# A transformer block with adaptive layer norm on one core: first loads in a new order, constant matmuls ahead of the first transposes, tiles turned through two banks, and a new shift table

## Chip, core and metric

The kernel runs on one core of a Trainium2 chip. Its time is the device time of one execution in microseconds (us). Before the change three runs gave 738.66, 738.86 and 739.36 us, a median of 738.86 us. The engines are called PE (TensorE, matrix products), DVE (VectorE), ACT (ScalarE), POOL (GpSimd) and SP (SyncE, which here only issues transfers). PEld is the loading of weights into PE.

## What is computed

The reference, cut to what matters (x is 2048 x 1024, all inputs are bfloat16):

```python
mod = (silu(c) @ w_mod).reshape(1, 6, 1, -1)
sa, ca, ga, sb, cb, gb = mod[:, 0] ... mod[:, 5]
h = layernorm(x) * (1 + ca) + sa
q, k, v = split(h @ wqkv)                 # 32 heads of 32
pq, pk = phi(q), phi(k)                   # phi(t) = t + 1 where t > 0, else exp(t); + 1e-6
o = (pq @ sum(pk^T v)) / (pq . sum(pk))   # linear attention
x = x + ga * (o @ wo)
h = layernorm(x) * (1 + cb) + sb
x = x + gb * ((gelu(h @ w_gate) * (h @ w_up)) @ w_down)
```

## The kernel before

The 2048 rows are worked in four blocks of 512, each of four tiles of 128 rows. The attention half takes the blocks in turn for k and v (`kvq_phase`, L1396) and then q, merges, and the feed-forward half takes two groups of 1024 rows. Many products are done by Strassen-like schemes with seven half products.

**A planner orders everything.** Each call on `te`, `ve`, `ac`, `gp`, `sy` only records an operation. `Plan.order` (L439) estimates start times with a cost model, forward and backward, and gives each operation a due time. PE's operations stay in program order; those of the other engines are ordered by due time, and loads are not issued more than a set time ahead of theirs. Two lists bend the due times: `plan.chain` and `plan.pairs` hold operations of which each must not be due before its predecessor. `plan.aim` ties an operation to a transfer. `Plan.refine` (L466) then applies the table `SHIFTS` (L20): for every engine a list of numbers, where position i of the final order takes the operation at position i + shift of the planner's. `zN` stands for N zeros. So a table fits only the list of operations that it was made for.

**The start** is `start_phase` (L936). It works block 0 without the scratch that the later blocks use:

- It loads four tiles of x (`load_x`, L780: 256 KB each), the columns of `w_mod` for ca in four quarters (`wm`, L947: 512 KB each, into `wm_ca`), the v columns of `wqkv` in four quarters (`wv` through L784, 512 KB each), the sa columns of `w_mod` (`ModRow`, L832: four of 512 KB), and the first half of the k columns `Wk` (L784, 1 MB). Before the change x1, x3 and one quarter of `wm_ca` go out on ACT's queue, as does c (L775), the rest on SP's.
- c is transposed on PE (L976) with `identb` (L974, a copy on DVE) and goes through silu to `scol`, a column for PE, and `srep`.
- The tiles are normalized: tiles 0 and 2 with bn_stats on DVE (`ln_rows`: L865, L867, then Ln and Exp on ACT, L878 and L879, and the scaling L894), tiles 1 and 3 with sums on ACT (`act_stats`: L884 to L887, and L991 on DVE).
- `start_tile` (L903) turns a tile with eight PE transposes (L906). The two halves of it go to two PSUM banks and are copied to `hs0` by DVE (L909) and ACT (L910). Two pairs of banks are used in turn, from a ring of four (`psT`).
- `scale_cols` (L927) makes 1 + ca for half of the channels with 32 products of one column each (L931), and L934 adds the 1. `scale_wv` (L912) multiplies a half or quarter of Wv by it (L914). I call the two halves' products SC0 and SC1.
- `v_plain` (L917) makes the v products of tile tl and column half n, in two halves over k (L922). I call them V with tile and column half, so V10 is tile 1, columns 0. L925 copies the results to `vta`.
- The row of sa is made by `ModRow.step` (L859) and turned to a column by `columns` (L845 to L852). Then hr1[0], the modulated input of the k products, is made with eight DVE operations, one for each slice of 128 channels (L1033).
- `keep_warm` (L898) issues matmuls whose result nobody reads.

After it `shift_row` (L1037) makes a row from sa and Wv (L859 again), and the k products of block 0 follow (`k_group`, L1249).

**Block 1** comes from `ln1_block(1)` (L1054): x4 to x7 are loaded, normalized (stats on DVE at L865, POOL at L872 to L1063, ACT at L1065), stored to a DRAM scratch (L1066, on POOL's queue), turned by a DMA transpose (L1067, on SP's queue) and scaled by DVE (L1070). It is recorded after `start_phase`. Before the change its loads are put into `plan.chain` among those of the start. Its v products are L1150, its k products L1249.

PE's order before the change, read from its table: transpose of c, tile 1, two `keep_warm`, tile 0, first half of SC0, tile 2, second half of SC0, V10, tile 3, V20, first half of SC1, V00, V30, V01, second half of SC1, and the other V products. The second half of V11 (L922 at 43.47) comes only among the k products.

Of the kernel before, what the change touches and what calls it, by code (L numbers as in the profile page):

```python
# [21 lines left out]
        "z1 40 40 40 40 40 40 40 40 48 48 -10 -10 -10 -10 -10 -10 -10 -10 -10 -10 -10 -10 -10 -10 -10 -10 -10 -10 -10 "  # L22
        "-10 -10 -10 -10 -10 18 18 18 18 10 10 10 10 -18 -18 -18 -18 -18 -18 -18 -18 -18 -18 -18 -18 -18 -18 -18 -18 4 "
        "4 4 4 16 16 16 16 8 8 8 8 -4 -4 -4 -4 12 12 12 12 12 12 12 12 12 12 12 12 12 12 12 12 -32 -32 -32 -32 24 24 24 "
        "24 -28 -28 -28 -28 z16 4 4 4 4 -40 -40 -40 -40 8 8 8 8 8 8 8 8 -4 -4 -4 -4 -12 -12 -12 -12 24 24 24 24 4 4 4 4 "
        "4 4 4 4 4 4 4 4 4 4 4 4 -20 -20 -20 -20 4 4 4 4 4 4 4 4 4 4 4 4 20 20 20 20 20 20 20 20 20 20 20 20 20 20 20 "
        "20 20 20 20 20 20 20 20 20 -12 -12 -12 -12 -12 -12 -12 -12 12 12 12 12 12 12 12 12 -36 -36 -36 -36 -36 -36 -36 "
        "-36 20 20 20 20 20 20 20 20 -4 -4 -4 -4 -4 -4 -4 -4 -96 -96 -96 -96 -8 -8 -8 -8 -8 -8 -8 -8 z8 16 16 16 16 16 "
        "16 16 16 16 16 16 16 16 16 16 16 -16 -16 -16 -16 -16 -16 -16 -16 8 8 8 8 48 48 48 48 -24 -24 -24 -24 -24 -24 "
        "-24 -24 -4 -4 -4 -4 -4 -4 -4 -4 33 33 33 33 28 3 3 3 3 3 3 3 3 11 11 11 11 -21 -21 -21 -21 -21 -21 -21 -21 -21 "  # L30
        "-21 -21 -21 8 8 8 8 33 33 33 33 33 33 33 33 z8 13 13 13 13 5 5 5 5 -41 -41 -41 -41 -41 -41 -41 -41 -11 -11 -11 "
        "-11 -19 -19 -19 -19 -24 16 16 16 16 16 16 16 16 16 16 16 16 16 16 16 16 -16 -16 -16 -16 -16 -16 -16 -16 -16 "
        "-16 -16 -16 -16 -16 -16 -16 4 4 4 4 36 36 36 36 z12 24 24 24 24 -24 -24 -24 -24 -8 -8 -8 -8 -8 -8 -8 -8 24 24 "
        "24 24 -12 -12 -12 -12 -12 -12 -12 -12 -12 -12 -12 -12 32 32 32 32 24 24 24 24 16 16 16 16 -8 -8 -8 -8 z4 -24 "
        "-24 -24 -24 -24 -24 -24 -24 -8 -8 -8 -8 -20 -20 -20 -20 28 28 28 28 -4 -4 -4 -4 16 16 16 16 -8 -8 -8 -8 -4 -4 "
        "-4 -4 -12 -12 -12 -12 -8 -8 -8 -8 8 8 8 8 8 8 8 8 -4 -4 -4 -4 4 4 4 4 8 8 8 8 -28 -28 -28 -28 -4 -4 -4 -4 4 4 "
        "4 4 -4 -4 -4 -4 4 4 4 4 -4 -4 -4 -4 z20 24 24 24 24 -4 -4 -4 -4 -4 -4 -4 -4 -4 -4 -4 -4 4 4 4 4 20 20 20 20 "
        "-12 -12 -12 -12 -12 -12 -12 -12 12 12 12 12 28 28 28 28 20 20 20 20 -16 -16 -16 -16 -16 -16 -16 -16 -16 -16 "
        "-16 -16 20 20 20 20 -12 -12 -12 -12 -12 -12 -12 -12 -12 -12 -12 -12 32 32 32 32 -8 -8 -8 -8 -8 -8 -8 -8 16 16 "
        "16 16 -8 -8 -8 -8 -4 -4 -4 -4 z4 36 36 36 36 -20 -20 -20 -20 z12 8 8 8 8 -32 -32 -32 -32 4 4 4 4 20 20 20 20 "  # L40
        "-16 -16 -16 -16 z4 -20 -20 -20 -20 z4 -8 -8 -8 -8 4 4 4 4 -4 -4 -4 -4 4 4 4 4 52 52 52 52 52 52 52 52 52 52 52 "
        "52 -16 -16 -16 -16 -8 -8 -8 -8 -16 -16 -16 -16 -12 -12 -12 -12 -12 -12 -12 -12 -12 -12 -12 -12 -12 -12 -12 -12 "
        "-12 -12 -12 -12 -12 -12 -12 -12 -12 -12 -12 -12 -12 -12 -12 -12 -12 -12 -12 -12 -12 -12 -12 -12 8 8 8 8 8 8 8 "
        "8 8 8 8 8 -12 -12 -12 -12 28 28 28 28 28 28 28 28 12 12 12 12 -8 -8 -8 -8 -8 -8 -8 -8 -8 -8 -8 -8 -8 -8 -8 -8 "
        "16 16 16 16 16 16 16 16 16 16 16 16 16 16 16 16 -56 -56 -56 -56 -24 -24 -24 -24 24 24 24 24 12 12 12 12 20 20 "
        "-22 -22 -22 -22 -30 -30 -30 -30 -6 -6 -6 -6 16 16 16 16 16 16 16 16 16 16 16 16 16 16 16 16 -8 -8 -8 -8 -8 -8 "
        "-8 -8 -38 -38 -38 -38 13 3 3 3 3 7 2 2 2 2 8 8 8 8 18 -1 -1 -1 -1 3 -50 -50 -50 -50 4 4 4 4 5 -5 -5 -5 -5 1 1 "
        "1 1 -14 14 -1 -1 -1 -1 1 1 1 1 6 z4 -10 -10 z4 6 6 6 6 6 6 6 6 -8 -8 -8 -8 -8 2 -9 -1 4 4 4 4 -4 -4 -4 -4 2 2 "
        "2 2 -4 -4 z4 40 40 40 40 40 40 40 40 24 24 24 24 24 24 24 24 48 48 48 48 48 48 48 48 24 24 24 24 24 24 24 24 "
        "24 24 24 24 24 24 24 24 -40 -40 -40 -40 -40 -40 -40 -40 -40 -40 -40 -40 -40 -40 -40 -40 -40 -40 -40 -40 -40 "  # L50
        "-40 -40 -40 -40 -40 -40 -40 -40 -40 -40 -40 z16 16 16 16 16 16 16 16 16 -8 -8 -8 -8 -8 -8 -8 -8 -8 -8 -8 -8 -8 "
        "-8 -8 -8 8 8 8 8 8 8 8 8 -8 -8 -8 -8 -8 -8 -8 -8 16 16 16 16 4 4 4 4 4 4 4 4 -12 -12 -12 -12 -12 -12 -12 -12 8 "
        "8 8 8 8 8 8 8 -8 -8 -8 -8 -8 -8 -8 -8 8 8 8 8 8 8 8 8 -8 -8 -8 -8 -8 -8 -8 -8 4 4 4 4 4 4 4 4 4 4 4 4 -12 -12 "
        "-12 -12 40 40 40 40 40 40 40 40 16 16 16 16 16 16 16 16 -12 -12 -12 -12 -20 -20 -20 -20 -16 -16 -16 -16 -16 "
# [449 lines left out]
def kernel(  # L504
# [14 lines left out]
    P = 128  # L519
# [1674 lines left out]
```

## Time and profile before

| what | value |
|---|---|
| median of the runs | 738.86 us |
| span of the profiled execution, first to last instruction | 737.0 us |
| median less span | 1.86 us |
| PE busy | 719.7 us (98%) |
| DVE busy | 652.0 us (88%) |
| ACT busy | 453.9 us (62%) |
| bytes moved | 159.27 MB, 216 GB/s |
| chain that ended last | PE 79%, DVE 14%, ACT 3% |

The profile is of one execution; its times count from the start of the span. No time of that execution outside its span is given, so the span is set beside the median of the runs. A group of instructions is named by the line that issued it, its engine and its operation; L787 is a helper (`tt_op`) that many steps share. The chain of work that ended last is followed back from the last instruction, each step to what released it. "Waits" are idle times of an engine before an instruction that another one released. Some records can be missing.

### The profile page before, as it was taken

The page shows a single profiled execution, that of the slowest core. Times are in us where ns is not written, and L with a number is a line of the kernel's source. Part 1 is how long each engine was busy: PE and PEld are TensorE (multiplying, and loading weights), DVE is VectorE, ACT ScalarE, POOL GpSimd, SP SyncE. Part 2 cuts the span into 40 slices and gives each one's busy share as a digit, 9 for nine tenths or more (in the row PEclk, how much of TensorE's full clock was granted, in tenths as well). Part 3 has the DMA queues.
Part 4 walks back from the last instruction along what each step waited for, and adds up shares of the span by engine and source line. Part 5 has one row for each costly group of instructions (what it writes and reads, how often), then busy time and mean ns, then how long its engine had stood idle before and what let it go on. Part 6 is the DMA issues. An engine that isn't in the chain of part 4 may idle for free.

```text
span 737.0 us, 12105 instructions
## 1 busy us (share of the span) xinstructions
PE 719.7 (98%) x4340; PEld 406.1 (55%) x4353; DVE 652.0 (88%) x1466; ACT 453.9 (62%) x827; POOL 98.6 (13%) x174
## 2 busy tenths in 40 slices
PE   4999999999999999999999999999999999999997
PEld 3444545444444455555555667555555555568774
DVE  6699898777799999999997598988897999999998
ACT  5377566569786889999876631026777776642010
POOL 2344471000020222112110000010000000000000
PEclk9999999999999999999999999999999999999999
DMA  9987994978698967655896897745343545698972
GB/s 315 356 215 222 222 185 112 325 277 223 199 212 245 320 223 242 203 161 209 235 237 217 242 282 242 244 148 177 107 125 114 172 136 180 196 283 248 284 236 73
DMA packets 160958, 159.27 MB, mean 216 GB/s; under 512 B 34177, under 2 KB 140417, under 8 KB 160257
## 3 DMA queue, kind: packets, MB, share of 16 engines
q1 hardware_dynamic: 142864, 121.52, 55.2%
q0 software_dynamic: 14848, 33.82, 15.3%
q10 hardware_dynamic: 3184, 3.15, 1.3%
q8 instruction: 34, 0.56, 0.3%
q14 instruction: 28, 0.22, 0.1%
HBM read 122.42 MB, written 36.04 MB: 215 GB/s over the span
## 4 chain that ended last, share of the span: by engine, by line
PE 79%; DVE 14%; ACT 3%; issue 2%; DMA 1%; POOL 0%; ACTq 0%; DVEq 0%; POOLq 0%
PE psum L1706 28%; DVE mem L787 12%; PE psum L1717 9%; PE psum L1922 7%; PE psum L1150 7%; PE psum L1220 7%; PE psum L1967 5%; PE psum L1527 4%; PE psum L1249 4%; PE psum L1591 3%; PE psum L922 2%; PE psum L1264 1%; ACT mem L1094 1%; DVE mem L2139 1%; DMA ts<-mem 1%
## 5 line engine op out<-in xcount | busy, mean ns | idle before, releaser
L787 DVE TENSOR_TENSOR mem<-mem 128x256 f16<-128x256 f16 (+13 forms) x857 | 376.8, 485 | 15.4 <-ACT mem L1791 3.3
L1706 PE MATMUL psum<-mem 128*128 128x512 f16 x1144 | 273.0, 379 | 0.1
L1094 ACT ACTIVATE mem<-psum 128x512 f32<-128x512 f32 (+3 forms) x320 | 168.1, 556 | 138.3 <-DVE mem L787 42.0
L787 DVE TENSOR_TENSOR mem<-psum,mem 128x512 f16<-128x512 f32 (+6 forms) x213 | 159.4, 756 | 31.3 <-PE psum L1220 4.9
L1706 PEld LDWEIGHTS <-mem 128*128 128x128 f16 (+1 forms) x1144 | 111.7, 98 | 104.3 <-issue 1.7
L1717 PE MATMUL psum<-mem 128*128 128x256 f16 x742 | 105.4, 272 | 0.1
L1717 PEld LDWEIGHTS <-mem 128*128 128x128 f16 (+1 forms) x742 | 72.4, 98 | 41.4 <-issue 1.3
L1967 PE MATMUL psum<-mem 128*128 128x256 f16 (+1 forms) x784 | 88.5, 273 | 0.1
L1967 PEld LDWEIGHTS <-mem 128*128 128x128 f16 x784 | 76.7, 98 | 12.7 <-issue 0.5
L1922 PE MATMUL psum<-mem 128*128 128x512 f16 (+2 forms) x348 | 75.7, 370 | 1.6 <-DVE mem L787 1.5
L1150 PE MATMUL psum<-mem 128*128 128x512 f16 (+1 forms) x274 | 62.7, 379 | 0.3
L787 DVE TENSOR_TENSOR psum<-psum,mem 128x256 f32<-128x256 f32 x106 | 44.4, 427 | 15.5 <-ACT mem L1094 13.9
L1922 PEld LDWEIGHTS <-mem 128*128 128x128 f16 x350 | 34.2, 98 | 37.0 <-issue 1.7
L1762 ACT ACTIVATE psum<-psum 128x512 f32<-128x512 f32 x56 | 32.7, 585 | 34.0 <-PE psum L1706 22.5
L1220 PE MATMUL psum<-mem 128*128 128x512 f16 x224 | 51.9, 379 | 0.0
L1150 PEld LDWEIGHTS <-mem 128*128 128x128 f16 x280 | 27.0, 98 | 31.0 <-issue 0.2
L1781 ACT ACTIVATE mem<-psum 128x512 f16<-128x512 f32 x56 | 33.3, 597 | 8.7 <-PE psum L1706 8.6
L1220 PEld LDWEIGHTS <-mem 128*128 128x128 f16 (+1 forms) x224 | 21.6, 98 | 26.1 <-issue 1.4
L1791 ACT ACTIVATE mem<-mem 128x512 f16<-128x512 f16 x56 | 34.8, 628 | 0.9 <-DVE mem L787 0.9
L1249 PE MATMUL psum<-mem 128*128 128x512 bf16 x123 | 28.5, 379 | 0.3
L1527 PE MATMUL psum<-mem 128*128 128x512 f16 x128 | 28.1, 379 | 0.0
L1328 POOL DMA_DIRECT2D ts<-in_B_w_down_dram x28 | 27.2, 1411 | 3.7 <-DMA ts<-in_B_w_down_dram 3.7
(142 smaller groups left out, 562.8 us busy)
## 6 DMA issues: line engine op xcount, KB each, us to landing
mem<-in_B_w_gate_dram SPq DMA_DIRECT2D x14, 1024.0 KB
mem<-in_B_w_up_dram SPq DMA_DIRECT2D x14, 1024.0 KB
mem<-in_w_mod_dram SPq DMA_DIRECT2D x23, 512.0 KB
mem<-us SPq DMA_DIRECT2D x24, 448.0 KB
mem<-ts SPq DMA_DIRECT2D x5, 1792.0 KB
ts<-in_B_w_down_dram POOLq DMA_DIRECT2D x28, 256.0 KB, 5.8
mem<-in_B_w_down_dram SPq DMA_DIRECT2D x15, 448.0 KB
mem<-in_A_x_dram SPq DMA_DIRECT2D x22, 256.0 KB
```

The lines of the kernel that those rows point to most:

```text
L787: ve.tensor_tensor(out=out, in0=a, in1=b, op=op)
L1094: ac.activation(out=t, in_=ps, func=AF.Copy)
L1150: te.matmul(ps, lhsT=A[:, k, i * P:(i + 1) * P], rhs=B[:, k, :], start=(start and k == 0), stop=(k == KH - 1), skip_group_check=True)
L1220: te.matmul(o, lhsT=W[:, k, (j0 + i) * P:(j0 + i + 1) * P], rhs=h_form(a, k), start=(start and k == 0), stop=(k == KH - 1), skip_group_che ...
L1249: te.matmul(ps, lhsT=hr1[b][:, k, tl * P:(tl + 1) * P], rhs=Wk[:, k, n * NW:(n + 1) * NW], start=(k == 0), stop=(k == KD - 1))
L1527: te.matmul(psw[:, half, :], lhsT=pqT[b][:, g, tl * P:(tl + 1) * P], rhs=Wp[:, g, half * NW:(half + 1) * NW], start=(g == 0), stop=(g == K ...
L1706: te.matmul(ps, lhsT=a[:, k, e, :], rhs=b[:, k, :], start=(start and k == 0), stop=(k == KH - 1), skip_group_check=True)
L1717: te.matmul(ps, lhsT=self.x[a][:, k, :], rhs=self.y[y][:, k, :], start=(start and k == 0), stop=(k == KH // 2 - 1), skip_group_check=True)
L1781: ac.activation(out=o, in_=ps, func=AF.Gelu_apprx_tanh)
L1791: ac.activation(out=o, in_=o, func=AF.Gelu_apprx_tanh)
L1922: te.matmul(psm[:, q, c], lhsT=A[:, i, q * P:(q + 1) * P], rhs=wt[:, i, c], start=(start and i == 0), stop=(i == NPR - 1), skip_group_chec ...
L1967: te.matmul(ps[:, q, :], lhsT=a[:, k, q * P:(q + 1) * P], rhs=y[:, k, :], start=(start and q == 0 and k == 0), stop=(k == NPR // 2 - 1), s ...
```

## The change

- `SHIFTS` is replaced for all five engines: PE has 4365 entries for 4353, DVE 1451 for 1453, ACT 805 for 804, POOL 153 as before, SP 224 for 223.
- Loads: the program order is now x0, x1, two quarters of `wm_ca`, one of Wv, x2, one of Wv, x3, the other two of `wm_ca`, the other two of Wv, sa, Wk, and then x4 to x7 (`first_x`), which `ln1_block(1)` takes over. x1 and x2 go out on ACT's queue, everything else on SP's, with c on ACT's as before. All entries in `plan.chain` and `plan.pairs` go, and the `plan.aim` of the start.
- `keep_warm` now multiplies the identity with itself, four copies side by side, so it needs no data. There are 8 of them ahead of the transpose of c, 4 ahead of tile 0 and 2 after it in the program (14 in all, 2 before), into bank 5 in place of bank 6.
- `start_tile` uses banks 0 and 1 for every tile. The banks of the V products change.
- The program order of the products changes, and tile 0 comes first. PE's order by the new table: 8 `keep_warm`, transpose of c, 6 `keep_warm`, first half of tile 0, SC0, second half of tile 0, tile 1, V00, V10, half of tile 2, V11, the other half, V01, tile 3, SC1, V20, and the others; all V products come before the k products.
- Two of the eight slices of hr1[0] (2 and 5) are made by ACT.

```diff
 SHIFTS = {
     "PE": (
-        "z1 40 40 40 40 40 40 40 40 48 48 -10 -10 -10 -10 -10 -10 -10 -10 -10 -10 -10 -10 -10 -10 -10 -10 -10 -10 -10 "
...
-    psT = Banks(0, 3)
-    psD, psS, psR = Banks(6, 6), Banks(7, 7), Banks(7, 7)
+    psD, psS, psR = Banks(5, 5), Banks(7, 7), Banks(7, 7)
...
-    def keep_warm(n, rhs):
+    def keep_warm(n):
 
         for _ in range(n):
-            te.matmul(psD(), lhsT=ident, rhs=rhs, start=True, stop=True, skip_group_check=True)
-
-    def start_tile(pss, tl, xh):
-
+            te.matmul(psD().rearrange("p (j n) -> p j n", j=4), lhsT=ident,
+                      rhs=ident[:, None, :].to_broadcast((P, 4, P)), start=True, stop=True, skip_group_check=True)
+
+    def start_tile(tl, xh):
+
+        ps = [psm[:, h, :].bitcast(F16)[:, 0:NW].rearrange("p (k t) -> p k t", t=P) for h in range(2)]
         for kd in range(KD):
-            te.transpose(pss[kd // 4][:, kd % 4, (tl % 2) * P:(tl % 2 + 1) * P], xh[:, kd * P:(kd + 1) * P],
-                         ident)
...
+            te.transpose(ps[kd // 4][:, kd % 4, :], xh[:, kd * P:(kd + 1) * P], ident)
+        ve.tensor_copy(out=hs0[:, 0:KH, tl * P:(tl + 1) * P], in_=ps[0])
+        ac.activation(out=hs0[:, KH:KD, tl * P:(tl + 1) * P], in_=ps[1], func=AF.Copy)
...
         x()
+        x(ac)
+        wm(0, 0)
+        wm(0, 1)
+        wv(0, 0)
+        x(ac)
+        wv(0, 1)
         x()
-        wm(0, 0)
-        x()
-        wm(0, 1)
-        x()
-        wv(0, 0)
-        wv(0, 1)
         wm(1, 0)
         wm(1, 1)
         wv(1, 0)
-        plan.pairs += [*zip(order, order[1:])]
         wv(1, 1)
-        plan.chain.append(plan.ops[-1])
-        plan.pairs.append((order[-2], order[-1]))
         sa = ModRow(0, wm_sa)
-        plan.chain += sa.loads
         load_w(Wk[:, :, 0:NW], D, NW)
+        first_x.extend(load_x(TT + tl) for tl in range(TT))
         ve.tensor_copy(out=identb[0:KD, :], in_=ident[0:KD, 0:KD])
+        keep_warm(8)
         pcc = psM(BF16)[:, 0:KD]
...
+        keep_warm(4)
+        start_tile(0, xh[0])
+        keep_warm(2)
         scale_cols(0, 0, KH, psc[0])
         scale_cols(0, KH, KD, psc[0])
-        start_tile(halves[1], 1, xh[1])
-        start_tile(halves[0], 2, xh[2])
-        keep_warm(2, xh[1][:, 0:NW])
+        start_tile(1, xh[1])
         scale_wv(0, 0)
...
         for kd in range(KD):
-            ve.tensor_scalar(out=hr1[0][:, kd, :], in0=hs0[:, kd, :], scalar1=opcA[:, kd:kd + 1],
-                             scalar2=modT[:, kd:kd + 1], op0=ALU.mult, op1=ALU.add)
+            if kd % 3 == 2:
+                ac.activation(out=hr1[0][:, kd, :], in_=hs0[:, kd, :], func=AF.Identity, scale=opcA[:, kd:kd + 1],
+                              bias=modT[:, kd:kd + 1])
+            else:
+                ve.tensor_scalar(out=hr1[0][:, kd, :], in0=hs0[:, kd, :], scalar1=opcA[:, kd:kd + 1],
+                                 scalar2=modT[:, kd:kd + 1], op0=ALU.mult, op1=ALU.add)
...
         for tl in range(TT):
-            xt = load_x(b * TT + tl)
-            if b == 1:
-                plan.chain.insert((1, 2, 5, 7)[tl], plan.ops[-1])
+            xt = first_x[tl] if b == 1 else load_x(b * TT + tl)
```

## The prediction, made before the change was run

> **What bounds the kernel now.** I read the page first, then the table of windows, then the chain of work that ended last in the first 80 us, then the timeline around block 1. The page and the table say that TensorE (PE) is the bound and where it is not busy:
>
> ```profile
> span 737.0 us, 12105 instructions
> ...
> PE 719.7 (98%) x4340; PEld 406.1 (55%) x4353; DVE 652.0 (88%) x1466; ACT 453.9 (62%) x827; POOL 98.6 (13%) x174
> ```
>
> ```profile
> 0.00:4.00 4.00, 0.00 (x0) 0.00 (x0) 0.66 (x13) 1.28 (x1) 3.05 (x19) 1.00 0.56 149
> 4.00:8.00 4.00, 0.22 (x2) 0.17 (x3) 2.96 (x8) 3.59 (x8) 0.52 (x3) 1.00 1.03 379
> 8.00:12.00 4.00, 3.57 (x38) 2.60 (x39) 3.42 (x11) 2.11 (x8) 0.00 (x0) 1.00 1.09 358
> 12.00:16.00 4.00, 2.57 (x27) 1.61 (x26) 3.33 (x11) 1.75 (x5) 1.34 (x3) 1.00 1.10 348
> 16.00:20.00 4.00, 4.00 (x33) 2.31 (x32) 1.94 (x6) 2.21 (x3) 0.00 (x0) 1.00 1.10 358
> 20.00:24.00 4.00, 4.00 (x35) 2.03 (x33) 1.58 (x8) 0.00 (x0) 0.57 (x2) 1.00 1.05 384
> ...
> 36.00:40.00 4.00, 4.00 (x20) 1.78 (x19) 4.00 (x9) 1.57 (x3) 0.00 (x0) 1.00 0.57 137
> ...
> 720.00:737.00 17.00, 11.50 (x77) 7.24 (x74) 13.38 (x26) 0.00 (x0) 0.00 (x0) 0.97 0.24 79
> ```
>
> Columns: window, its length, busy us of PE, PEld, DVE, ACT, POOL, granted clock, DMA share, GB/s. Of PE's 17.3 us of idle time (737.0 - 719.7) 9.6 us lie before 16 us and 5.5 us after 720. Between them it is idle for 2.2 us only, 1.1 of them at 142. So what the start saves reaches the end, if the other engines and the loads keep up. DMA is full from 4 to 36 us at about 0.36 MB per us; DVE is idle for 4.5 us between 16 and 24 but full from 32 to 50.
>
> The chain shows a second loss, the rate of the first products:
>
> ```profile
> 13.61 0.88 DVE mem L914 x3
> 14.54 1.87 PE psum L922 x4
> 16.40 0.85 PE psum L906 x8
> 17.26 1.71 PE psum L922 x4
> 18.96 0.40 PE psum L931 x16
> 19.36 2.61 PE psum L922 x12
> ```
>
> Start, length, what. Four products of 512 columns take 1.87 and 1.71 us, the next twelve 2.61 us, so 0.43 us each until about 19 us and 0.22 after. The granted clock column reads 1.00 throughout, so it does not show this: the rows' durations do. Last, the timeline where block 1 begins:
>
> ```profile
> 31.53 0.61 POOL L1066 DMA_DIRECT2D xas<-mem  x1 [0.59 <-ACT mem L1065]
> ...
> 36.76 4.04 SPq L1067 DMA_TRANSPOSE mem<-xas  x1
> ...
> 46.47 2.67 DVE L1070 TENSOR_SCALAR mem<-mem 128x512 f16<-128x512 f16 x8
> ```
>
> Block 1's rows go through a scratch and a DMA transpose; the scaled result is there from 46.5 to 49.1, and PE begins on it at 48.65 (v products, L1150) and 49.5 (k products, L1249, which read all eight slices). PE shows no wait, but the cover is only 0.3 to 0.8 us.
>
> **The change part by part.** The program order of PE is PE's base order, so the shift table gives its new order: 8 constant matmuls, the transpose of c, 6 more constant ones, half of tile 0, all 32 column products of SC0 (L931), the rest of tiles 0 and 1, then V products. The other engines' base order comes out of the planner and can't be read from the diff.
>
> Constant matmuls, 14 for 2. They need only the identity, which POOL finishes at 1.4 us, and PE's first work so far is at 6.50, so 8 at 0.43 us (two took 1.06 with their drain) end near 5.2. The transpose of c then follows; c landed by 4.71, and its other operand, L974, ran late at 6.31 because DVE had three bn_stats ahead of it. If it follows at 5.4, six more end at 8.0; at 6.5 and still slow, at 9.2. Cost: 0 to 1.3 us; I take 0, since tile 0 isn't ready before 7.9 either.
>
> Tile 0 first. x0 landed by 4.50; two bn_stats (1.89/3 each) and L867 (0.21) end at 6.0; ACT has x1's two passes until 6.74, then Ln and Exp (0.24 and 0.17 by L878, L879); L894 takes 0.55: 7.9, where tile 1 stood before (7.94). Half a tile at 0.107 per transpose is 0.43, 32 column products at 0.026 are 0.85, so SC0 ends at 9.2 in place of 13.1. It no longer stands behind tile 2, which waited for ACT's copy. The loads: before, eight transfers went out and the ninth (L947, 4.30) only when x1 landed; now both wm_ca halves are within the first eight and x4 to x7 are not. By the rates above 1.75 MB are in at 7.0, 2.75 MB (with both Wv quarters sharing the engines) at 9.8; SC0's second half needs them at 8.7. Cost 0 to 1.2, taken 0.
>
> Two banks. Each tile's half now waits for the copy of the half before it. T0hi and T1hi stand together, so PE waits once for ACT: the chain has 0.65 us from such a copy's start to the next transpose (11.04 to 11.69). T0hi 0.43 + 0.65 + T1 0.86 puts V00 at 11.1; the DVE path (0.2 for L934, 1.23 from its end to the first product, as 13.31 to 14.54) gives 10.8. I take 11.0 against 14.54: **3.5 us**.
>
> Rate. If PE is at 0.22 us when V00 starts, the excess goes: 1.87 - 0.87, 0.85 - 0.45, 1.71 - 0.87 make **2.2 us**. If not, 0.
>
> Added on the path: tile 2 now comes after V00, 0.45 us at the full rate. V11's second half moves ahead of the K products, 0.86 us from one place to another, net 0.
>
> Waits inside the V stretch. From V00 to the shift row (L859, 32.12) lay 17.6 us; now 17.6 - 2.2 + 0.45 + 0.86 = 16.7, so 27.7 without waits. Two floors: the mod row (sa) loads need 8 MB if x4 to x7 go first, and DMA had moved 7.9 MB by 24; sa's products would stand at 23.8. And DVE's rows from 4.5 us to the last hr1 slice at 33.6 add up to 20 us, 6 of them block 1's stats, which would now have to fit before 30. I charge **1.0 us**, bounds 0 and 3.
>
> hr1 split: two of eight slices go to ACT, 0.33 each off DVE and (half of L1065's 1.24) 0.65 each onto ACT. PE reads slice 2 only after 0.98 us of row sums, which hide it; without that cover it costs up to 0.7, and it gives at most 0.7. Taken 0.
>
> Block 1. To use the head start, x4 to x7 must be loaded, normalized, stored and turned about 3.5 us earlier than now. Their stats need not wait: DVE stood idle 4.07 us for the late second half of SC1, which now comes right after tile 3. I charge **0.5 us**, bounds -0.5 and 6.5.
>
> The rest of the new table reorders every engine to the end. PE's new order moves groups by 5 to 30 places and ends in the same 42 products; PE has 2.2 us of waits to lose between 16 and 720, and could gain as many. Taken 0, bounds -1.5 to 2.
>
> Sum: -3.5 - 2.2 + 0.45 + 1.0 + 0.5 = -3.75. The span would be 733.25. The times shown lie 1.86 us over the profiled span (738.86 - 737.0; the profiled execution has no time of its own in the results), so **735.1**.
>
> **The rivals.** *The rate is still low at V00.* For it: between 7.94 and 13.11 PE ran 24 transposes, 32 small products and two constant ones, and tile 3 at 16.20 still took 0.107 per transpose; only after 4.4 us of wide products did the rate rise. Between the last constant matmul and V00 lie 3 us of just such small work. Against it: 14 wide ones ahead, some 6 us. Its price is the 2.2 us: 737.3. [...]
>
> *Block 1 is late.* In the program x4 to x7 now stand after Wk. Should they go out there, 9 MB are in at 27.0; x7's stats began at 25.96 before, and 20.5 us later DVE began to scale. With stats from 27.4, in a stretch where DVE is full, so 1 to 3 us later still, scaling begins at 49 to 51, and PE has nothing else that doesn't need it. It decides from 47.3 on (46.5 plus the 0.8 of cover); at the middle PE starts 2.7 us later than now, less what order can hide: 741.3, slower. Against it: SP was free to load them before, and DMA has room.
>
> *The head start is given back.* DVE, full from 32 to 50 with sums that wait for the shift row, doesn't finish them earlier: block 1 starts where it did, and nothing after it is shorter: 738.9.
>
> *Everything fits.* Without the 1.5 us charged and with some waits gone: 733.0 or a little less.
>
> **How the numbers follow.** Forecast (733.6 to 736.8) 0.45; low rate 0.15; block 1 late (739.5 to 743) 0.20; given back 0.12; everything fits 0.08. The range 732.2 to 740.6 leaves out a little of the last and over half of the late block. A difference of 0.2% (1.5 us) is about what a measurement of this kernel can tell from none. Faster by more: 0.45 + 0.08 + 0.11 of the low rate = 0.64; within: 0.04 + 0.10 = 0.14; slower: 0.20 + 0.02 = 0.22.
>
> **What would show it.** SC0's last product near 9.2; V00 near 11 at 0.22 each (0.43: the first rival); the shift row near 28.7; DVE's L1070 counterpart before 43.5 with no PE wait ahead of block 1 (at 47.3 or later: the second rival); PE's idle time between 16 and 720 near 2 us. It would be wrong if wm_ca lands after 9, if the constant matmuls push tile 0 past 8, or if waits appear in the middle that the old table didn't have.

## The result, and the profile after

The changed kernel takes **768.74 us** (median of 4 runs, 768.54 to 771.15) beside 738.76 us for the kernel before on the same chip: the ratio is 1.0413, with a 95% interval of 1.0398 to 1.0429. It is slower by 30 us where 3.75 us less had been forecast, far outside the range.

```profile
span 767.0 us, 12099 instructions
...
PE 730.9 (95%) x4353; PEld 405.7 (53%) x4365; DVE 656.0 (86%) x1464; ACT 456.1 (59%) x829; POOL 101.1 (13%) x174
```

The page of the changed kernel: PE is busy for 11 us more and idle for 36.1 us (767.0 - 730.9) in place of 17.3. The start did what the prediction said, nearly. In the timeline of PE (start, length, line, tile; in brackets the idle time before it and what ended it):

```profile
5.12 2.11 PE L907 MATMUL psum<-mem 128*128 128x512 f16 x6
7.07 0.39 PE L914 MATMUL psum<-mem 128*128 128x128 f16 x4
7.30 0.54 PE L937 MATMUL psum<-mem 128*128 128x1 bf16 x16
8.02 0.55 PE L937 MATMUL psum<-mem 128*128 128x1 bf16 x16 [0.18 <-DMA mem<-in_w_mod_dram]
...
10.45 1.03 PE L914 MATMUL psum<-mem 128*128 128x128 f16 x8 [1.64 <-DVE mem L989]
11.28 2.89 PE L928 MATMUL psum<-mem 128*128 128x512 f16 x8
```

SC0 ends at 8.57 and V00 starts at 11.28, against 14.54 before. The same stretch in the table of windows (columns as in the prediction):

```profile
8.00:12.00 4.00, 2.34 (x30) 1.76 (x31) 3.83 (x12) 3.79 (x11) 0.00 (x0) 0.74 1.10 356
12.00:16.00 4.00, 4.00 (x23) 1.91 (x22) 2.33 (x7) 1.92 (x5) 0.00 (x0) 0.84 1.10 352
16.00:20.00 4.00, 3.98 (x53) 2.38 (x52) 2.67 (x10) 1.07 (x3) 0.00 (x0) 1.00 1.07 372
36.00:40.00 4.00, 3.75 (x17) 1.54 (x16) 3.90 (x8) 4.00 (x9) 0.96 (x2) 1.00 0.52 197
180.00:190.00 10.00, 6.12 (x23) 2.31 (x21) 5.64 (x10) 4.86 (x7) 0.00 (x0) 0.83 0.67 233
```

The granted clock fell to 0.50 at 9.9 us and was back at 1.00 at 13.3, so V00 and V10 ran partly at the low rate. Block 1 is scaled from 45.62 us on, 0.85 us earlier than before:

```profile
45.62 2.68 DVE L1066 TENSOR_SCALAR mem<-mem 128x512 f16<-128x512 f16 x8 [0.88 <-DMA mem<-xas]
```

The last row of the windows is new: at 180 us PE stands still and then runs at a reduced clock (0.83 over the row's 10 us). The table of waits says for what (in all, times, longest):

```profile
PE psum L1713 <- DVE mem L793: 4.4, 4, 2.0
PE psum L1523 <- DVE mem L793: 4.2, 2, 3.3
PE psum L1305 <- DVE mem L793: 3.9, 1, 3.9
PE psum L1702 <- DVE mem L793: 3.5, 4, 1.4
PE psum L1963 <- DMA mem<-in_B_w_down_dram: 3.5, 1, 3.5
```

L793 is the helper `tt_op` (L787 before); L1305, L1523, L1702 and L1963 are products from 150 us to the end. Nothing of this kind stood in the profile before: behind 20 us its PE waited 1.1 and 1.5 us for DVE and for no transfer.

```profile
PE psum L1922 <- DVE mem L787: 1.5, 1, 1.5
PE psum L1264 <- DVE mem L787: 1.1, 1, 1.1
```

To see where the time goes I set PE's progress in each run beside that of the kernel before: the time at which it has started equally many of the operations that both have, less the time before (the lag), as a median over the 25 us that begin at the time given. Negative is ahead. In the first three columns, where the orders of PE differ most, the lag shifts by up to 0.8 us with the choice of operations that are counted.

| us in the kernel before | 25 | 50 | 100 | 150 | 175 | 200 | 225 | 275 | 350 | 425 | 525 | 625 | 700 |
|---|---|---|---|---|---|---|---|---|---|---|---|---|---|
| changed kernel | -2.3 | -1.5 | -1.1 | -2.9 | 1.9 | 4.4 | 9.2 | 11.7 | 16.9 | 23.2 | 27.1 | 27.7 | 30.8 |
| old kernel, new loads (below) | 0.2 | 0.2 | 0.0 | 5.1 | 5.1 | 13.7 | 13.7 | 13.7 | 25.7 | 26.1 | 34.2 | 39.1 | 44.7 |
| changed kernel, seven places mended | -2.7 | -1.8 | -1.5 | -3.2 | -2.6 | 0.3 | 2.7 | 3.7 | 10.3 | 10.8 | 15.7 | 16.6 | 19.3 |
| old kernel, one place spoilt | 0.4 | 0.4 | 0.2 | 0.2 | 6.2 | 6.2 | 6.2 | 6.2 | 6.1 | 6.1 | 6.1 | 6.1 | 6.1 |
| best version | -2.7 | -2.9 | -1.8 | -1.8 | -1.8 | -1.8 | -1.8 | -1.8 | -1.9 | -1.9 | -1.9 | -1.9 | -1.9 |

The changed kernel is ahead until its first long wait, at 180.6 us, and then loses 33.7 us up to 700 us (from -2.9 to 30.8) in steps. Its trace has 16 PE waits of over 0.6 us behind 166 us, 26.1 us in all (the kernel before has one, of 1.5), and three drops of the clock of 3.41 us each (a "window" in the expectations), which begin in the last 0.2 to 0.7 us of the waits of 3.88, 3.26 and 3.52 us. The granted clock is 0.50 in them, so they cost half of what lies behind the waits, an estimated 4.4 us in all. So 26.1 - 1.5 + 4.4, some 29 us of the 32.9 that are lost from 150 us to the end of the span (2.9 + 30.0), are these. The first of them, on DVE and on PE:

```profile
174.83 1.22 DVE L793 TENSOR_TENSOR mem<-psum,mem 128x1024 f16<-128x1024 f32 x1 [0.32 <-PE psum L1216]
181.98 0.69 DVE L793 TENSOR_TENSOR mem<-mem 128x1024 bf16<-128x1024 bf16 x1 [5.93 <-DMA mem<-den]
182.59 0.42 DVE L1085 TENSOR_SCALAR mem<-mem 128x1024 f16<-128x1024 f16 x1
183.12 1.90 DVE L793 TENSOR_TENSOR mem<-mem 128x1024 bf16<-128x1024 f16 x3
```

```profile
177.84 2.75 PE L1216 MATMUL psum<-mem 128*128 128x512 f16 x12
184.47 1.04 PE L1305 MATMUL psum<-mem 128*128 128x512 f16 x2 [3.88 <-DVE mem L793]
185.29 2.92 PE L1216 MATMUL psum<-mem 128*128 128x512 f16 x8
```

DVE stands for 5.93 us at a product that reads the transfer of `den`. Behind it in DVE's order are three operations that had what they read at 175.0, 178.7 and 162.9 us; PE's L1305 needs one of them. Eight products then take 2.92 us instead of 1.89: the granted clock is 0.50 from 184.0 to 187.4.

### The profile page after: what moved, and what is told of

Read it like the earlier page. It is cut to its first block, busy times and chain, and to the rows that moved or that the text cites. A ratio compares the mean times of both kernels' runs of the same rounds, so it can differ in the third digit from the quotient of the medians.

```text
span 767.0 us, 12099 instructions
## 1 busy us (share of the span) xinstructions
PE 730.9 (95%) x4353; PEld 405.7 (53%) x4365; DVE 656.0 (86%) x1464; ACT 456.1 (59%) x829; POOL 101.1 (13%) x174
## 4 chain that ended last, share of the span: by engine, by line
PE 36%; DMA 12%; issue 9%; DVE 8%; SPq 2%; POOL 1%; ACT 0%; DVEq 0%; POOLq 0%
PE psum L1702 24%; PE psum L1713 8%; DVE mem L793 7%; DMA mem<-in_B_w_up_dram 2%; SPq L1953 2%; PE psum L1963 2%; DMA us<-mem 2%; DMA mem<-ts 1%; PE psum L1918 1%; DMA mem<-x2s 1%; DMA x2s<-mem 1%; DMA vs<-mem 1%; DMA mem<-us 1%; DMA mem<-in_B_w_down_dram 1%; DMA mem<-in_B_w_gate_dram 1%
## 5 line engine op out<-in xcount | busy, mean ns | idle before, releaser
L793 DVE TENSOR_TENSOR mem<-mem 128x512 f16<-128x512 f16 (+9 forms) x857 | 379.1, 485 | 34.8 <-DMA mem<-den 9.2
L1702 PE MATMUL psum<-mem 128*128 128x512 f16 x1144 | 275.5, 379 | 3.6 <-DVE mem L793 3.5
L793 DVE TENSOR_TENSOR mem<-psum,mem 128x512 f16<-128x512 f32 (+6 forms) x213 | 159.7, 756 | 29.1 <-PE psum L1963 5.7
L1702 PEld LDWEIGHTS <-mem 128*128 128x128 f16 (+1 forms) x1144 | 111.6, 98 | 107.2 <-issue 4.8
L1713 PE MATMUL psum<-mem 128*128 128x256 f16 x742 | 108.0, 272 | 6.6 <-DVE mem L793 4.4
L1963 PE MATMUL psum<-mem 128*128 128x256 f16 (+1 forms) x784 | 89.9, 275 | 5.3 <-DMA mem<-in_B_w_down_dram 3.5
L1963 PEld LDWEIGHTS <-mem 128*128 128x128 f16 x784 | 77.0, 99 | 18.9 <-issue 3.8
L793 DVE TENSOR_TENSOR psum<-psum,mem 128x256 f32<-128x256 f32 x106 | 44.3, 427 | 14.9 <-ACT mem L1090 12.0
L1918 PEld LDWEIGHTS <-mem 128*128 128x128 f16 x350 | 34.3, 98 | 39.1 <-issue 3.8
L1216 PE MATMUL psum<-mem 128*128 128x512 f16 x224 | 52.7, 384 | 0.0
L1146 PEld LDWEIGHTS <-mem 128*128 128x128 f16 x280 | 27.1, 98 | 31.3 <-issue 0.2
L1523 PE MATMUL psum<-mem 128*128 128x512 f16 x128 | 29.9, 391 | 4.2 <-DVE mem L793 4.2
L1324 POOL DMA_DIRECT2D ts<-in_B_w_down_dram x28 | 28.9, 1034 | 0.6 <-issue 0.4
```

Of the source, the lines that this page charges most:

```text
L793: ve.tensor_tensor(out=out, in0=a, in1=b, op=op)
L1146: te.matmul(ps, lhsT=A[:, k, i * P:(i + 1) * P], rhs=B[:, k, :], start=(start and k == 0), stop=(k == KH - 1), skip_group_check=True)
L1216: te.matmul(o, lhsT=W[:, k, (j0 + i) * P:(j0 + i + 1) * P], rhs=h_form(a, k), start=(start and k == 0), stop=(k == KH - 1), skip_group_che ...
L1523: te.matmul(psw[:, half, :], lhsT=pqT[b][:, g, tl * P:(tl + 1) * P], rhs=Wp[:, g, half * NW:(half + 1) * NW], start=(g == 0), stop=(g == K ...
L1702: te.matmul(ps, lhsT=a[:, k, e, :], rhs=b[:, k, :], start=(start and k == 0), stop=(k == KH - 1), skip_group_check=True)
L1713: te.matmul(ps, lhsT=self.x[a][:, k, :], rhs=self.y[y][:, k, :], start=(start and k == 0), stop=(k == KH // 2 - 1), skip_group_check=True)
```

## The experiments

All times are medians; the ratio is to the kernel before on the same chip, with its 95% interval. The edits are entries of `SHIFTS` (position i takes the operation at i + shift); in the diffs the first character of a line is the sign.

### Which part of the new order costs the time?

**New start, old order behind it** (e1), **old start, new order behind it** (e2), **new order up to 166 us** (e3), **new start and the planner's own order behind it** (e4). The first entries that differ, for SP:

```diff
 e1, "SP" from place 19 of the changed kernel (176 of 224 entries differ)
-4 0 -2 -1 6 -2 -1 2 5 -2
+0 9 2 -2 -2 2 -3 -2 1 4
 e2, "SP" from place 18 of the kernel before (176 of 223)
-0 9 2 -2 -2 2 -3 -2 1 4
+4 0 -2 -1 6 -2 -1 2 5 -2
 e3, "SP" from place 52 of the changed kernel (146 of 224)
-5 -8 6 7 -10 6 3 18 28 -11
+13 -8 -8 9 -2 -7 -1 -10 -1 -3
 e4, "SP" from place 19 of the changed kernel (178 of 224)
-4 0 -2 -1 6 -2 -1 2 5 -2
+0 0 0 0 0 0 0 0 0 0
```

> The changed kernel's code with a table that keeps its new order up to the last operation of the start on each engine (195 of PE, 59 of DVE, 49 of ACT, 19 of SP) and has the order of before for everything behind it. Theory (the order behind the start costs the 30 us, the start itself saves 2 to 3.5): 735 to 737 us. Rival A (the new start itself causes the later stalls, through loads that come at other times): over 760. Rival B (an order fits only the start that it was made for): 742 to 760.

Measured: 752.37 us, 1.0188 (1.0172 to 1.0203).

> The kernel before with a table that keeps its order up to the last operation of the start on each engine and has the new order behind it. Theory (the order behind the start costs it): 770 to 773 us, since the 2 to 3.5 us of the start are missing too. Rival A (the new start is at fault): 738 to 740. Rival B (an order fits only its own start): also slow, and by more than the changed kernel, so this run alone does not tell B from the theory; e1 does.

Measured: 772.99 us, 1.0461 (1.0433 to 1.0489).

> The changed kernel with its new order for all that it starts up to about 166 us (959 of PE's operations) and the order of before behind that. PE is 1 to 2 us ahead of before there by the two traces, and the first stall of 3.9 us comes at 184. Theory (what is lost is lost by the order behind 166 us): 736 to 738.5. Rival (some state left by the earlier part, such as late stores or loads, causes the later stalls): over 750.

Measured: 743.31 us, 1.0067 (1.0050 to 1.0084).

> The changed kernel with its order up to the last operation of the start, and no shifts behind it: the planner's own order. If the new table was made well for this program and only the program is worse, this is slower than the changed kernel's 768.7, by tens of us. If the new table behind the start is no better than none, it is at 755 to 770. My guess is 775 to 800.

Measured: 786.70 us, 1.0653 (1.0632 to 1.0674).

e2 settles that the start isn't the cause: with the old start the new order behind it loses as much, in much the same steps (level with the kernel before to about 1 us up to 150 us, 12 behind at 225, 31.4 at 700). e1 and e3 came out above what was expected, e1 in the range of rival B, and their traces say why: all of it is lost within some 35 us behind the place where the two orders meet. In e1 the two hr1 slices on ACT stood behind ACT operations of the old order:

```profile
30.83 0.60 PE L1245 MATMUL psum<-mem 128*128 128x512 bf16 x2
40.75 3.59 PE L1245 MATMUL psum<-mem 128*128 128x512 bf16 x8 [9.31 <-ACT mem L1028]
```

From 50 us on e1 stays 14.3 to 14.5 us behind, from 200 us e3 5.4 us, both to the end: the old order runs as well when it begins late. That rules out that an order fits only its own start. e4, 18 us slower than the changed kernel, doesn't show that the new table is better than none: its PE waits 6.66, 4.75 and 4.84 us ahead of 70 us, and from 75 us to 700 it loses 28.4 us more, where the changed kernel loses 31.8. Behind the start the new table was no better than the planner's own order.

### Can the orders meet without loss?

**New order up to 46 us** (e5) and **up to 90 us** (e6), cut where nothing before the cut needs anything behind it.

```diff
 e5, "SP" from place 24 (171 of 224 entries differ)
--2 -1 2 5 -2 -2 0 -6 1 -2
+2 -3 -2 1 4 -2 -5 -1 -1 0
 e6, "SP" from place 35 (162 of 224)
-8 -1 4 -1 -3 2 -1 -3 -5 0
+3 -1 2 -2 4 -3 1 -2 13 -3
```

> The changed program with its new order up to about 46 us (PE 275 operations, DVE 79, ACT 49, POOL 17, SP 23, a set that needs nothing from outside it) and, on every engine, the old order for all that is left. Theory (the start saves 2 to 3 us, the order behind it loses 32): PE's progress runs 2 to 3 us ahead of the kernel before from 50 us to the end, so 735.5 to 737 against 738.4, ratio 0.996 to 0.998, PE stalls beyond 50 us near the 5 us of the kernel before. Rival (an order fits only its own start, and two orders can't be joined without a loss of the size seen at the earlier seams, 8 and 14 us): 742 or more, with the loss right at 46 to 60 us and a constant lag behind it. Rival (head start is given back): 738.4.

Measured: 737.71 us, 0.9989 (0.9980 to 0.9998).

> As the run with the seam at 46 us, with the seam at about 90 us (PE 523, DVE 184, ACT 85, POOL 59, SP 34 operations in the new order). The changed kernel itself stood 1.0 to 1.5 us ahead there. Theory: the new order between 46 and 90 us gives back about 1 us of the head start and nothing is lost at a seam where both orders have done nearly the same work: 737 to 738, ratio 0.998 to 1.000. Rival (a seam costs 5 us or more wherever it lies): 742 or more. If it comes out at the time of the 46 us seam, the new order in between costs nothing.

Measured: 738.00 us, 0.9991 (0.9982 to 0.9999).

No loss of several us at such a cut, and 31 us less than the changed kernel: the loss is the order behind 90 us. e6 came out as expected; e5 gained less than that. What is kept is 0.8 to 1.1 us of the 2 to 3.5 that the start is ahead.

### Is it the loads, or DVE?

**The kernel before with the new table's load order behind the start** (e7), nothing else changed:

```diff
 "SP" from place 18 of the kernel before (176 of 223 entries differ)
-0 9 2 -2 -2 2 -3 -2 1 4 -2 -5 -1 -1
+4 0 -2 -1 6 -2 -1 2 5 -2 -2 0 -6 1
```

> The kernel before with one thing changed: SP issues the transfers behind the start in the order of the new table (176 of 223 places hold another transfer); all other engines keep the old order. If the loads of the new table alone make the loss (DVE waits 23 us for transfers in the changed kernel against 2.7 before): 755 to 772, with waits of DVE and PE on transfers behind 170 us. If it is the order of the other engines, above all DVE's, which puts operations ahead of the landing of what they read: 738 to 741, no waits on transfers over 1 us behind the start.

Measured: 781.17 us, 1.0575 (1.0551 to 1.0599): more than either side expected. On DVE of e7:

```profile
134.04 0.69 DVE L787 TENSOR_TENSOR mem<-psum,mem 128x512 f16<-128x512 f32 x1
140.32 0.42 DVE L787 TENSOR_TENSOR mem<-mem 128x512 f16<-128x512 bf16 x1 [5.59 <-DMA mem<-in_B_w_down_dram]
```

This load goes out at 135.8 in place of 125.4 us, because in SP's order it now stands behind one that waits for its buffer. So a load order can cost all of the loss. Is it then bad by itself? Three tries to mend the changed kernel's order by rule: **the old load order** as far as the other engines' orders allow it (e9), **loads ordered by need** as the trace shows it (e10), and **DVE by need as well** (e11).

```diff
 e9, "SP" from place 19 (174 of 224 entries differ)
-4 0 -2 -1 6 -2 -1 2 5 -2
+0 9 2 -2 -2 2 -3 -2 1 4
 e10 and e11, "SP" from place 20 (174 of 224)
-0 -2 -1 6 -2 -1 2 5 -2 -2
+-1 -1 2 -1 4 4 1 -1 -7 1
 e11, "DVE" from place 61 (1331 of 1451)
-3 66 3 29 13 -4 15 0 0 67
+17 66 6 29 30 -4 4 69 -5 5
```

> The changed kernel with one engine's order changed: behind the start SP issues its transfers in the old order wherever the other engines' new order allows it (55 pairs of transfers stand otherwise than in the old order, 485 do in the changed kernel). DVE, PE, ACT and POOL as in the changed kernel. Theory A (the new load order is bad by itself: it cost 42 us in the kernel before, and the changed kernel's 32 us are the same thing): the old order repairs most of it, 740 to 750. Theory B (an order of loads is good or bad only beside the compute order that it was made for; the fault of the new table is that its engines were not fitted to each other's true times): no repair, 765 or more, with DVE and PE waiting for transfers again.

Measured: 820.19 us, 1.1106 (1.1071 to 1.1141).

> The changed kernel with SP's order behind the start made anew from its own profiled execution: each transfer goes out when what it overwrites or reads is done there (4 us added for a transfer it waits for), at most 25 us before its first user started, the most urgent first. Other engines as in the changed kernel. If transfers that stand in the queue behind a waiting one make the loss: DVE's 23 us and PE's 7 us of waits for transfers go mostly, 745 to 757. If not the queue but DVE's order makes it (its operations put ahead of landings that no queue order could make earlier, such as den): 762 to 770.

Measured: 780.23 us, 1.0560 (1.0540 to 1.0580).

> As the run with loads by need, and DVE's order behind the start also made anew from the changed kernel's profiled execution: at each moment the operation that was ready there and whose first user started earliest. If the loss is the loads and in-order DVE together: 740 to 752, lower than with the loads alone by what DVE's order costs. If the loss lies in the order of PE itself (which neither run touches): both near 765.

Measured: 810.55 us, 1.0960 (1.0929 to 1.0991).

All three are slower than the changed kernel; my theory that one engine's order was bad by itself fell. The old loads, good in the old kernel, cost 51 us more beside the new compute order (PE waits 15.4 us at 219). By e7 and e9, an order of loads is good or bad only beside the orders of the other engines. The whole order of PE or of DVE wasn't exchanged by itself, so which of them the loads don't fit stays open.

### Is the loss a sum of single places?

**Two stalls mended** (e8): in the changed kernel the products that wait for `den` go behind ready operations of DVE. **Five more places mended** (e14), on top of that.

```diff
 e8, "DVE" places 315-321 and 357-362
-9 -2 0 -6 7 1 2   and   8 27 7 -6 -5 -5
+-1 -4 0 3 4 4 5   and   -3 -2 -2 5 24 4
 e14, on top: "SP" places 50-64 (127-130 and 205-218 likewise), "DVE" 681-689 (422-427 likewise)
-3 -4 5 -8 6 7 -10 6 3 18 28 -11 -8 2 -15   and   -3 11 0 -16 -13 -5 -3 8 -3
+-3 -6 -6 -3 -5 -2 1 3 4 4 1 16 26 -9 1   and   12 1 3 12 -7 -18 -15 -7 -5
```

> The changed kernel with 13 places of DVE's order changed: at 182 us and at 219 us the operations that wait for a transfer (den) are moved behind three ready ones (first place: the denominators after the phi products and the weighted rows that PE's L1305 needs; second: after the residual sum that PE's L1523 bank waits for). Nothing else. Theory (in-order DVE stands behind a late transfer, PE stands behind DVE, and each PE stall of over 3.3 us also halves the clock for 3.41 us, a loss of 1.7 us): PE's waits of 3.88 us at 180.6 and 3.26 us at 219 shrink to under 1 us, the two drops of the clock at 184 and 221.5 go, and the kernel gains 7 to 10.5 us: 758 to 762 in place of 768.7. Rival (the two stalls only show where a chain that is late anyway surfaces): the stalls come back within 40 us and the gain is under 3 us: 766 to 769.

Measured: 767.97 us, 1.0388 (1.0362 to 1.0414). The median lies in the rival's range; the four executions spread from 764.10 to 769.24, so a small gain is not clear of the noise. The profiled execution, the fastest of them, shows that both waits and their drops of the clock had gone, but 5 us behind the first a new one stood in its place, with a drop of its own (24 products took 2.72 us, where 32 of this line took 1.91 in the changed kernel at 190.52). (The 3.3 us of the expectation, from which a wait would cost clock, is too long: 3.26 us was enough at 219 and 3.04 here.)

```profile
185.42 0.62 PE L810 MATMUL psum<-mem 128*32 128x512 bf16 x8
189.07 2.72 PE L810 MATMUL psum<-mem 128*32 128x512 bf16 x24 [3.04 <-DMA mem<-in_w_mod_dram]
```

This load had a free buffer at 152 to 154 us. SP's queue in the changed kernel (start, length of issuing):

```profile
155.32 1.18 SPq L802 DMA_DIRECT2D mem<-in_w_mod_dram  x2
165.05 0.77 SPq L1283 DMA_DIRECT2D den<-mem  x1
165.89 0.80 SPq L802 DMA_DIRECT2D mem<-in_w_mod_dram  x1
...
179.00 0.33 SPq L802 DMA_DIRECT2D mem<-in_w_mod_dram  x1
```

SP stands from 156.5 to 165 at a store of `den` whose data isn't there, and five loads stand behind it. In e14 they go out ahead of it:

```profile
155.00 3.63 SPq L802 DMA_DIRECT2D mem<-in_w_mod_dram  x7
164.73 1.83 SPq L1283 DMA_DIRECT2D den<-mem  x2
```

> The changed kernel with the 13 places of DVE's order at 182 and 219 us changed as before (768.0), and five more places: SP issues five loads of w_mod, whose buffers are free at 152 to 154 us, ahead of the den store for which it stands idle until 165.4 (they went out at 166 to 181, and PE waited 3.03 us for one at 186); SP issues one load of w_down (buffer free at 407.4, issued 424.1, PE waited 2.55 us) and one near the end (free at 692, issued 717.9, PE waited 1.92 us) when their buffers are free; DVE takes three ready operations ahead of one that waits for the store of us at 366 us (PE waited 1.98 us) and one ahead of another at 257 us (PE waited 1.04 us). Theory (the loss of the new table is a sum of such single places, each worth its PE wait and, above 2 us or so, half a clock window of 1.7 us): 10.5 us of waits and 5.1 us of clock go; not all of it, since part surfaced elsewhere the first time: 754 to 762. Rival (the chain behind is late anyway): 765 to 769.

Measured: 758.87 us, 1.0286 (1.0259 to 1.0312). That is in the expected range: about 10 us of the 30 are back with 60 of 6998 entries changed. The third row of the table above shows where: 8 us up to 275 us and some 6 from 350 to 425. At 350 the mend failed: PE's wait of 1.98 us became one of 3.60 (at 365), with a drop of the clock.

The counterpart, **one such place put into the kernel before** (e15): one product that reads `den` stands nine places earlier on DVE.

```diff
 "DVE" places 316-325 of the kernel before
-2 -1 -5 0 3 3 -1 -3 -2 1
+10 1 -2 -6 -1 2 2 -2 -4 -3
```

> The kernel before with one operation of DVE put nine places earlier: one of the four den products, which read a transfer issued until 174.9 us, stands at 175.7 us instead of 185.1, ahead of what PE needs at 179.0. Nothing else. This is the pattern of the changed kernel's stall at 180.6 us put into a kernel that had none. Theory (one such place costs PE its wait and then a half clock window, and an otherwise tuned order neither makes it worse nor gives it back): DVE waits 5 to 6.5 us for den, PE 4 to 5 us near 179, the clock falls for one window, and PE's lag stays constant from 190 us to the end: 743.5 to 746. Rival (the cost of such a place is swallowed by slack behind): under 740; rival (it grows as later places go wrong): over 750.

Measured: 745.91 us, 1.0103 (1.0088 to 1.0118); the profiled execution took 744.70. DVE, then PE:

```profile
175.20 0.69 DVE L787 TENSOR_TENSOR mem<-mem 128x1024 bf16<-128x1024 f16 x1
181.89 0.69 DVE L787 TENSOR_TENSOR mem<-mem 128x1024 bf16<-128x1024 bf16 x1 [6.00 <-DMA mem<-den]
```

```profile
178.75 0.59 PE L1309 MATMUL psum<-mem 128*128 128x512 f16 x2
183.77 5.20 PE L1220 MATMUL psum<-mem 128*128 128x512 f16 x16 [4.43 <-DVE mem L787]
```

The same products in the kernel before:

```profile
178.98 3.68 PE L1220 MATMUL psum<-mem 128*128 128x512 f16 x16
```

PE waits 4.43 us, and the 16 products behind take 5.20 us where they took 3.68: 6.0 us from one operation, and the lag stays at 6.1 to 6.2 us to the end. Nothing later gives it back. By the medians the price is 7.5 us (745.91 against 738.45). The other three executions had mean granted clocks of 0.993 to 0.995, the profiled one 0.998; one or two more drops of 3.41 us at 0.50 would make that difference by an estimate (3.41 / 2 / 742.9 is 0.0023 for each), but they have no trace.

### Can the start's gain be kept?

**Three small edits in e6's first 42 us** (e12): PE turns tile 0 whole ahead of SC0 and spreads the constant matmuls; DVE and ACT take ready operations first. **Block 1 earlier** (e13) and, apart from it, **two statistics ahead of five sums** (e16; on ACT x7's scaling goes ahead of two copies), both on top of e12.

```diff
 e12, "PE" places 11-18 (35-62 likewise), "DVE" 9-17, "ACT" 31-41
-0 0 8 8 -2 -2 -2 -2   and   -3 0 1 2 3 -1 4 1 1   and   -3 7 9 6 6 -2 -12 -8 -2 -4 -6
+2 2 2 2 2 2 2 2   and   5 -4 -1 1 -1 2 2 2 2   and   8 8 -5 8 6 -2 0 -2 -4 -15 -11
 e13, "DVE" places 44-57 (ACT 23-33 and POOL 9-15 likewise)
-6 -15 -14 4 -6 9 2 -18 3 0 0 -10 0 -9
+-14 -13 -13 3 -6 -4 -2 0 6 -1 1 -2 -2 -1
 e16, "DVE" places 59-69, "ACT" 31-33
-1 -1 3 66 3 29 13 -4 15 0 0   and   8 8 -5
+34 9 -1 -3 1 64 1 12 -5 14 -1   and   -3 7 7
```

> The version with the seam at 90 us (738.0 against 738.8) with three small edits in the first 42 us. PE: both halves of tile 0 ahead of SC0, and of the 14 constant matmuls two between the halves of SC0 and two in the gap ahead of tile 1 (1.14 us idle, then four products at 0.43 us). DVE: the copy of tile 0's first half ahead of x2's statistics, tile 1's scaling ahead of the statistics' last step, SC0's four slices in the order in which V00 reads them. ACT: the first two K copies ahead of the pass for which ACT stood idle for 1.96 us. If these waits and the clock are what the start still loses: V00 starts near 10.8 in place of 11.4, its products run at 0.22, PE's waits of 0.21 and 1.04 us at 38.5 and 41.4 go, 735 to 737. Rival (block 1, which is scaled at 46.5 us in the kernel before as in the version with the seam at 90 us, holds all head start): 738, with a new PE wait of 1 to 2.5 us ahead of block 1's first product.

Measured: 738.33 us, 0.9996 (0.9988 to 1.0005). V00 started at 10.32 at the full clock (1.000 over the profiled execution; V00 and V10 took 2.16 us, 2.89 in the changed kernel), some 3.8 us ahead at 25 us, and PE waited 1.11 us ahead of block 1: the rival.

> The version with three small edits in the first 42 us (738.3 against 738.7; its profiled execution was 3.8 us ahead at 25 us, lost 0.84 at 22, 1.11 ahead of block 1 at 45.4 and 0.74 at the seam at 90), and behind it block 1 made earlier: DVE does x6's and x7's statistics in the 1.64 us in which it stood idle for the sa row and ahead of hr1, ACT takes x7's scaling 3 us earlier, POOL stores each tile as soon as it is scaled. Theory (the head start is real and was held back by block 1's chain of statistics, store, transposing transfer and scaling): block 1's scaling starts near 43.5 in place of 46.1, PE's wait ahead of block 1 goes, lag of -2.5 to -3 at 50 us, and what is kept at the end is 1 us more than in the version it comes from: 737 to 737.5. Rival (the loads of x6 and x7 land too late for that, so the sa row and hr1 get late): 738.5 to 740, with a wait of DVE for x at 25 us.

Measured: 738.39 us, 0.9998 (0.9990 to 1.0006). The rival again, just under its range: DVE waited 1.85 us for x6 at 26.8, which made the sa row late, and block 1's scaling still began at 46.0. But this trace and e12's showed something else: POOL, which prepares x7, was slow beside DVE's sums. In e12, POOL and then DVE:

```profile
31.93 0.75 POOL L878 TENSOR_SCALAR mem<-mem 128x1 f32<-128x1 f32 x1
32.76 0.86 POOL L879 TENSOR_TENSOR mem<-mem 128x1 f32<-128x1 f32 x1
33.72 1.33 POOL L1059 TENSOR_SCALAR mem<-mem 128x1 f32<-128x1 f32 x1
```

```profile
31.92 3.08 DVE L793 TENSOR_TENSOR mem<-mem 128x1024 f16<-128x1024 bf16 x5
```

> The version with three small edits (738.3 against 738.7) with one more: DVE takes two statistics of later tiles (0.68 us each) ahead of the five 1024-wide sums at 31.9 us in place of behind them, and ACT takes x7's scaling ahead of the first two K copies. In that version POOL's one-column operations for x7 took 0.75, 0.86 and 1.33 us between 31.9 and 35.0 us, while DVE ran these sums, and 0.25 to 0.59 us elsewhere. Theory (the sums hold POOL up, POOL holds x7's scaling, and with it block 1): POOL's three operations take 0.25, 0.57 and 0.27 us, x7's scaling starts 1 to 1.9 us earlier than 35.1, block 1's scaling before 45.2 in place of 46.1, and PE's wait of 1.11 us ahead of block 1 goes: 737.2 to 737.8. Rival (POOL's operations are slow for another reason, or the statistics wait for their loads): no change, 738.3.

Measured: **736.62 us, 0.9978 (0.9969 to 0.9987)**, faster than both kernels. POOL and DVE of e16:

```profile
32.04 0.23 POOL L878 TENSOR_SCALAR mem<-mem 128x1 f32<-128x1 f32 x1
32.35 0.57 POOL L879 TENSOR_TENSOR mem<-mem 128x1 f32<-128x1 f32 x1
33.02 0.27 POOL L1059 TENSOR_SCALAR mem<-mem 128x1 f32<-128x1 f32 x1
```

```profile
32.02 1.27 DVE L871 BATCH_NORM_STATS2 mem<-mem 128x6 f32<-128x512 bf16 x2
33.21 3.07 DVE L793 TENSOR_TENSOR mem<-mem 128x1024 f16<-128x1024 bf16 x5
```

Block 1's scaling on DVE, in e12 and then in e16:

```profile
46.08 1.06 DVE L1066 TENSOR_SCALAR mem<-mem 128x512 f16<-128x512 f16 x3 [2.48 <-DMA mem<-xas]
```

```profile
43.84 2.67 DVE L1066 TENSOR_SCALAR mem<-mem 128x512 f16<-128x512 f16 x8
```

POOL's three operations take 1.07 us in place of 2.94, and ACT's scaling of x7, which waits for the third of them, starts at 33.32 in place of 35.08. Block 1's scaling starts at 43.84 in place of 46.08, and PE's wait ahead of it is gone. The gain is 0.6 us more than expected. Of the lead at 25 us (2.7 us in the table) 1.9 remain at the end.

## Why the prediction was wrong

- **The step that failed**: "The rest of the new table reorders every engine to the end. [...] Taken 0, bounds -1.5 to 2." It measured about +32 (33.7 us by PE's progress from 150 to 700 us; e2, with the old start, 31.4), as PE waits and drops of the clock from 180 us on. That is the last of the prediction's own signs of being wrong, waits in the middle that the old table didn't have. The reason given, that PE has only 2.2 us of waits to lose, bounds the gain; nothing bounded the loss. The profile before showed DVE at 88% busy, SP's queue full of loads that wait for buffers (those of L1667 stood 105.7 us in all for PE's L1706), and hardly any PE wait: an order that looked to have little slack. A row for the price of a wrong place was missing, and I put a small number where I should have put a wide one. e15 gives that price: 6.0 us for one operation (7.5 by the medians).
- **V00 at 11.0, worth 3.5**: 11.28, 3.26 us. Right. SC0's end came at 8.57, forecast 9.2.
- **Rate, 2.2**: half right. The granted clock was 1.00 from 6.5 to 9.8, 0.50 from 9.9 to 13.3 and 1.00 behind it. V00 and V10 took 2.89 us, where eight such products take 1.90 at 26.50 in the same trace. So about 1.2 of the 2.2 us came. Tile 1's transposes ahead of V00 were slow too: 1.03 in place of 0.62 in e12. The rival "the rate is still low" gave a reason that fits, the small work ahead of V00; beside it PE was idle for 1.64 us, and which of the two let the clock fall isn't shown.
- **Waits in the V stretch, 1.0**: the shift row stood at 29.60 (forecast 28.7, before 32.12), 18.3 us behind V00 where 16.7 without waits had been forecast. About 1.0 of the 1.6 us is the low rate of V00 and V10, already in the line above; the timeline shows one wait, of 0.24 us. So the waits were charged too high.
- **Block 1, 0.5**: its scaling began at 45.62, 0.85 us earlier than before; forecast was before 43.5. PE's lag there is -1.5 us. The rival "block 1 is late" did not come about as priced (47.3 or later); the one that came is "the head start is given back", in part and for another reason than DVE's sums being late themselves: they hold POOL (shown by e16; in the changed kernel the same three operations of POOL took 0.75, 0.87 and 1.33 us). ACT also kept PE waiting 1.04 us at 40.
- Up to 150 us, then, the sum (-3.75) was 1 to 2.7 us too good, and the sign right. The sign of the whole hung on the last term.

What stays open: e14 is still 20 us slower than the kernel before, with 10 PE waits of over 0.6 us left behind 166 us (14.9 us in all); that these are more places of the same kind is what the traces look like, but I mended no more of them. That the loss behind 90 us comes from the new order is shown (e2, e5, e6); that it is a sum of single wrong places is shown for about 10 of its 30 us. Why the new table has them can't be seen in the kernel.

## What to carry to other kernels

- Where each engine follows a written order (DVE stood 5.93 us at one product, with three operations behind it that had what they read), a change of that order is priced by the wrong places it may hold, not by the idle time it could win: one operation in front of a late transfer cost 6.0 us here (7.5 by the medians), and no slack behind gave it back.
- Orders of several engines belong together. Keep a known order for all that the change doesn't touch, join it where nothing ahead of the cut needs anything behind it (738.0 against 768.7 us), and mend single places from the trace.
- For a head start, look for the first thing that it can't move: here x7's way through POOL.

## What the runs showed of the hardware

- **The clock and the length of a wait.** In all 18 traces of this study, PE waits behind 30 us and ahead of the last 10 us, and how many had a drop of the granted clock begin in them or within 3.6 us of their end: 1.0 to 1.5 us, none of 51; 1.5 to 2, 2 of 13; 2 to 2.5, 3 of 8; 2.5 to 3, 4 of 5; 3 to 3.5, 6 of 9; longer, 29 of 29. A drop lasted 3.41 us or a multiple; those of the changed kernel were to 0.50. In that kernel the waits of 3.88, 3.52 and 3.26 us had one, those of 1.99 and 1.74 had none; over all traces, waits from 1.98 us on had one at times.
- **DVE's sums hold POOL.** A one-column operation on POOL (L1059) that takes 0.27 us took 1.33 beside DVE's 1024-wide sums in e12, and 3.50 in e13, where it ran from 32.24 to 35.74 and five such sums from 32.61 to 35.70, one behind the other. Beside the statistics, in e16, it took 0.27. Over all traces of the changed code, 98 operations of this line that didn't overlap such a sum took 0.26 to 0.43 us, and 70 that did took 0.26 to 3.50, with a median of 0.89. In e13 POOL's operation ended only with the last of the five sums. By which means a sum holds POOL, and why some operations were not held, no run shows.
